# Causal beacon attention with a quick-GELU MLP on one core: direct loads of all values, whole scratch writes, a fixed order of products

## The chip, the cores and the metric

The kernel runs on one core of one Trainium2 chip. Time is the device time of one execution in microseconds. Of 13 executions of the kernel before the median is 384.38 us (381.3 to 387.05). The profile is of one execution of 385.87 us, whose span from the first to the last instruction is 384.2 us.

## The reference

There are 8 batches, 8 heads, 576 positions of 64 elements, and 16 beacon keys and values per head that stand ahead of the others and are seen by every query.

```python
k_all = np.concatenate([beacon_k, k], axis=2)      # (8, 8, 592, 64)
v_all = np.concatenate([beacon_v, v], axis=2)
scores = scale * np.matmul(q, k_all.transpose(0, 1, 3, 2))
scores = np.where(causal, -1000000000.0, scores)   # causal over the 576, beacons always seen
a = np.exp(scores - scores.max(-1, keepdims=True))
a /= a.sum(-1, keepdims=True) + 1e-09
attn_out = np.matmul(a, v_all)
x = attn_out.transpose(0, 2, 1, 3).reshape(4608, 512)
h = x @ w_in                                       # (4608, 2048)
out = (h * (1.0 / (1.0 + np.exp(-1.702 * h)))) @ w_out
```

All inputs and the output are float32 in memory; the kernel loads them to float16 and accumulates in float32.

## The kernel before

**Attention.** The work is cut in 32 steps, step i being one pair of heads of one batch (four steps a batch). Scores are made transposed: keys on partitions, queries in the free dimension. `qk_chunk` (line 355) makes them in four chunks for both heads of the pair, from kT and qT that hold one head in partitions 0 to 63 and the other in 64 to 127. `exp_chunk` (line 368, ScalarE) turns each chunk into E, and `mask_chunk` cuts the diagonal blocks on GpSimd (line 391) or VectorE (line 384). `av_half` (line 425) multiplies E with the values, whose tile vb has 64 columns of values beside 64 columns of ones, so that the sums come out of the same product. Then come the copy out of PSUM (`av_out`, line 436), the turn of the sums (`z_turn`, 448), the reciprocal (454), the turn back (`z_back`, 458) and the multiplication into xT (`norm`, 467). These are VectorE's, except that some copies go to ScalarE.

**MLP.** Tokens are cut in nine groups of 512. Group g has sixteen first products of four matmuls each (`mlp1`, 494), sixteen gelus on ScalarE (506) and four second products of sixteen matmuls (`mlp2`, 516), each followed by a copy and a store of 256 KB (`mlp2_out`, `mlp2_store`). A group may start when the batches that it holds are normalized. ScalarE loads another function table when it goes from exponentials to gelus and back.

**q and k.** For batches 0 and 1 they come in long rows (`load_qk6`, six positions in a row), and TensorE transposes them (`tr_pe`, 179) through PSUM with copies by `tr_pe_out` (187). For batches 2 to 7 VectorE turns 32 by 32 squares (`tr_squares`, 277), VectorE or GpSimd puts them in order (`tr_order`, 286), and SyncE writes the result to scratch memory (`tr_write`, 297) and reads it back to where it belongs (`tr_place`, 303).

**Values.** For batches 2 to 7 `load_v` (231) loads them with rows of one head and position. For batches 0 and 1 `load_v6` brings them in long rows into the tile of the second weight, which is not filled yet, and `v_pe` (204) sends each row to its partition by products with a 0/1 matrix (`spread`, made on GpSimd); beacon values are added by a product with the identity (208). Ten copies (226) bring them from PSUM to vb. The second weight's first three quarters wait for the last of these products.

**What sets the order.** All of the kernel is a list of `Work` items with an engine (or a choice), a planned duration, a key and the items that they need or follow. `issue` is a list scheduler: it repeatedly takes the item with the earliest planned start, counting engines, buffers (`Buf`, with `rings` as the numbers of buffers) and a planned DMA time, and so writes every engine's instruction order by hand ahead of the run. On the chip, engines run their orders strictly and wait on semaphores; the planned times decide nothing else. Items of key 1e6 are warm-up products (`warm`, 916) that fill planned gaps of TensorE. Loads are issued by GpSimd, whose masks stand in the same order; scratch transfers and stores are issued by SyncE. A load from GpSimd reuses one of eight semaphores, so it waits for the eighth before it.

A few lines that a sentence doesn't say:

```python
ends = [min(NPAIR * (((g + 1) * GT - 1) // S) + LAG, NSTEP) for g in range(NG)]   # 6 10 14 18 22 26 30 32 32
```

`ends[g]` is the step whose exponentials follow group g's gelus.

Of the kernel before, what the change touches and what calls it, by code (L numbers as in the profile page):

```python
# [9 lines left out]
F16 = mybir.dt.float16  # L10
# [6 lines left out]
def kernel(  # L17
# [34 lines left out]
    NBV = 2  # L52
# [27 lines left out]
    make_identity(nc, ident)  # L80
    keep = cst.tile([P, P + Nb], F16, tag="keep", name="keep")
    spread = cst.tile([TP, NKPAD + TR + 2], F16, tag="spread", name="spread")
    bkn = cst.tile([Nb, NB2, H, D], F16, tag="bkn", name="bkn")
    bvn = cst.tile([Nb, NBV, H, D], F16, tag="bvn", name="bvn")
# [13 lines left out]
    def make_spread():  # L98

        nc.gpsimd.affine_select(  # L100
            out=spread,
            in_=spread,
            compare_op=ALU.not_equal,
            fill=1.0,
            base=-Nb - TR,
            pattern=[[1, NKPAD + TR + 2]],
            channel_multiplier=-TR,
        )

# [9 lines left out]

# [3 lines left out]
    for t in kTs:  # L123
        nc.vector.memset(t[:, :, NK:NKPAD], 0.0)
# [21 lines left out]
    vflat = w2t.rearrange("p a n -> p (a n)")  # L146

    def load_qk6(b, g, w):
        if b not in nat6:
            nat6[b] = gp.tile([TP, 2, H, TR * D], F16, tag="g", name="g")  # L150
        nc.gpsimd.dma_start(
            out=nat6[b][:, w, g * HG : (g + 1) * HG, :],
            in_=(q, k)[w][b, g * HG : (g + 1) * HG].rearrange("h (p t) d -> p h (t d)", t=TR),
        )

    def v6(b):
        n = H * TR * D
        return vflat[0:TP, b * n : (b + 1) * n].rearrange("p (h t d) -> p h t d", h=H, t=TR)

    def load_v6(b):  # L160
        nc.gpsimd.dma_start(
            out=v6(b).rearrange("p h t d -> p h (t d)"),
            in_=v[b].rearrange("h (p t) d -> p h (t d)", t=TR),
        )

    def load_beacons(t, src):
        nc.gpsimd.dma_start(
            out=t.rearrange("n b h d -> n (b h) d"),
            in_=src[0 : t.shape[1]].rearrange("b h n d -> n (b h) d"),
        )  # L170
# [30 lines left out]

    vu = {}

    def v_pe(b, j):
        u = psu.tile([P, H * D], F32, tag="u", name="u")
        vu[(b, j)] = u
        if j == 0:
            nc.tensor.matmul(
                u[:, :],
                ident[0:Nb, :],  # L210
                bvn[:, b, :, :].rearrange("n h d -> n (h d)"),
                start=True,
                stop=False,
            )
        for t in range(TR):
            nc.tensor.matmul(  # L216
                u[:, :].rearrange("r (h d) -> r h d", h=H),
                spread[:, j * P - t + TR : (j + 1) * P - t + TR],
                v6(b)[:, :, t, :],
                start=(t == 0 and j > 0),  # L220
                stop=(t == TR - 1),
            )

    def v_pe_out(b, j, eng):
        r = min(P, NK - j * P)
        copy[eng](
            out=vbs[b % 2][0:r, j, :, 0:D],
            in_=vu[(b, j)][0:r, :].rearrange("r (h d) -> r h d", h=H),
        )

    def load_v(b, j, h0, h1):
        vb = vbs[b % 2]
        if j == 0:
            nc.gpsimd.dma_start(
                out=vb[0:Nb, 0, h0:h1, 0:D],
                in_=beacon_v[b, h0:h1].rearrange("h n d -> n h d"),
            )
            nc.gpsimd.dma_start(
                out=vb[Nb:P, 0, h0:h1, 0:D],
                in_=v[b, h0:h1, 0 : P - Nb, :].rearrange("h n d -> n h d"),  # L240
            )
        else:
            lo = j * P - Nb
# [50 lines left out]
    def tr_write(b, g, w, e):  # L294
        if e == 0:
            dqk[(b, g, w)] = dr.tile([2, P, QKW[w]], F16, tag=f"d{w}", name=f"d{w}")
# [654 lines left out]
```

The softmax here doesn't subtract the row's maximum and nothing guards it: scores larger than these inputs give would overflow.

## Time and profile before

| what | value |
|---|---|
| median of 13 executions | 384.38 us |
| the profiled execution | 385.87 us, span 384.2 us |
| TensorE busy | 367.9 us (96%) |
| VectorE busy | 266.5 us (69%) |
| ScalarE busy | 226.3 us (59%) |
| GpSimd busy | 146.5 us (38%) |
| scattering products of values (216) | 13.6 us in 60 matmuls |
| warm-up products (916) | 6.4 us in 18 matmuls |
| q0, the loads from GpSimd | 42816 packets, 18.62 MB |
| q1, SyncE's transfers | 18048 packets, 23.79 MB |

The engines are PE (TensorE), DVE (VectorE), ACT (ScalarE), POOL (GpSimd) and SP (SyncE). A busy time is the union of an engine's instructions in the profiled execution; ends of matmuls are modelled. PEclk is the granted clock of TensorE. A table by stage gives, for each stretch, the busy time and number of instructions of each engine, then the clock, the busy share of 16 DMA engines, and what they moved. In the chain of waits each row is a start, a duration, and an engine with the tile and line that it worked on.

### The profile page before, as it was taken

The numbers are of one execution on the slowest core, as the hardware profiler recorded it, in microseconds if no ns is written. First come the engines' busy times: TensorE is split into PE (matmuls) and PEld (weight loads), VectorE is DVE, ScalarE is ACT, GpSimd is POOL, SyncE is SP. The second block draws the span as 40 slices with busy tenths as digits, with TensorE's granted clock in tenths as the row PEclk, the third lists the DMA queues.
The fourth block names the chain that finished last, engine by engine and source line by source line (L and its number), as shares of the span: only waits on it lengthen the run. The fifth ranks groups of instructions, "written<-read, shape, count | busy, mean of one in ns | idle before, by whom it ended". The sixth has DMA issues, their size and how long they took to land.

```text
span 384.2 us, 6119 instructions
## 1 busy us (share of the span) xinstructions
PE 367.9 (96%) x2328; PEld 181.2 (47%) x2328; DVE 266.5 (69%) x443; ACT 226.3 (59%) x334; POOL 146.5 (38%) x263
## 2 busy tenths in 40 slices
PE   7897999889999999999999999999999999999995
PEld 3454445434445444444445774545444544444442
DVE  6468999389977997699859985998595458000021
ACT  1876866627674777477746766586648563735300
POOL 8455772326533752466235724472321030000000
PEclk9998999989999999999999999999999999999999
DMA  8999998746955794559465947494400011000012
GB/s 110 200 205 154 135 180 118 167 142 116 130 138 137 142 129 128 149 116 149 128 158 95 156 118 178 89 147 108 143 27 30 0 56 46 10 27 27 15 68 82
DMA packets 60892, 42.79 MB, mean 111 GB/s; under 512 B 32192, under 2 KB 53184, under 8 KB 60864
## 3 DMA queue, kind: packets, MB, share of 16 engines
q0 software_dynamic: 42816, 18.62, 40.8%
q1 hardware_dynamic: 18048, 23.79, 20.3%
q8 instruction: 18, 0.29, 0.3%
q14 instruction: 10, 0.08, 0.1%
HBM read 44.40 MB, written 16.61 MB: 159 GB/s over the span
## 4 chain that ended last, share of the span: by engine, by line
PE 58%; DVE 28%; ACT 7%; issue 3%; DMA 3%; POOL 0%; SPq 0%; ACTq 0%; DVEq 0%
PE u L494 28%; PE u L516 18%; DVE xT L467 6%; DVE zt L448 6%; PE u L425 5%; DVE O L436 5%; ACT E L368 4%; PE s L355 3%; DVE sq L277 3%; DVE rz L458 3%; ACT L368 2%; DVE osb L529 2%; PE u L216 2%; PE u L916 2%; DMA n<-in_k_dram 1%
## 5 line engine op out<-in xcount | busy, mean ns | idle before, releaser
L368 ACT ACTIVATE E<-s 128x1024 f16<-128x1024 f32 (+3 forms) x128 | 104.0, 867 | 60.4 <-PE s L355 35.4
L494 PE MATMUL u<-xT,w 128*128 128x512 f16 (+1 forms) x640 | 133.6, 358 | 2.5 <-DVE O L436 1.6
L516 PE MATMUL u<-w,g 128*128 128x512 f16 x576 | 131.1, 383 | 2.8 <-DVE O L436 2.8
L506 ACT ACTIVATE g<-u 128x512 f16<-128x512 f32 x144 | 83.9, 598 | 53.0 <-PE u L494 52.9
L391 POOL TENSOR_SCALAR_AFFINE_SELECT E<-E 128x256 f16<-128x256 f16 (+2 forms) x147 | 58.4, 415 | 132.2 <-ACT E L368 131.6
L494 PEld LDWEIGHTS <-w 128*128 128x128 f16 x640 | 60.2, 98 | 60.1 <-issue 6.7
L516 PEld LDWEIGHTS <-g 128*128 128x128 f16 x576 | 55.1, 99 | 68.9 <-issue 5.4
L529 DVE COPY osb<-u 128x512 f32<-128x512 f32 x30 | 20.4, 681 | 74.9 <-PE u L516 74.8
L425 PE MATMUL u<-E,vb 128*128 128x336 f16 (+4 forms) x448 | 56.5, 270 | 0.8 <-DVE qT L187 0.7
L436 DVE COPY O<-u 128x240 f32<-128x240 f32 (+1 forms) x103 | 42.2, 432 | 14.9 <-PE u L425 13.4
L467 DVE TENSOR_TENSOR xT<-O,rz 64x576 f16<-64x576 f32 x64 | 51.8, 810 | 0.8
L448 DVE STREAM_TRANSPOSE zt<-O 64x576 f32<-64x576 f32 x64 | 49.3, 770 | 1.7 <-ACT O L436 0.2
L425 PEld LDWEIGHTS <-vb 128*128 128x128 f16 (+1 forms) x448 | 38.7, 99 | 20.7 <-issue 4.7
L355 PE MATMUL s<-qT,kT 64*128 64x80 f16 (+5 forms) x384 | 39.1, 284 | 3.8 <-ACT E L368 2.5
L286 POOL COPY t<-sq 128x576 f16<-128x576 f16 x24 | 29.1, 1211 | 32.0 <-DVE sq L277 31.6
L277 DVE STREAM_TRANSPOSE sq<-n 128x576 f16<-128x576 f16 x48 | 35.2, 752 | 4.7 <-POOL E L391 3.5
L355 PEld LDWEIGHTS <-kT 64*128 64x128 f16 x384 | 14.3, 94 | 33.1 <-issue 26.1
L286 DVE COPY t<-sq 128x576 f16<-128x576 f16 x24 | 27.3, 1136 | 0.2
L458 DVE STREAM_TRANSPOSE rz<-rt 128x576 f32<-128x576 f32 x32 | 24.4, 764 | 0.5
L245 POOL DMA_DIRECT2D vb<-in_v_dram x24 | 21.3, 893 | 0.0
L216 PE MATMUL u<-w,spread 96*128 96x512 f16 x60 | 13.6, 380 | 0.0
L436 ACT COPY O<-u 128x336 f32<-128x336 f32 (+1 forms) x25 | 10.4, 424 | 2.4 <-PE u L425 2.2
(49 smaller groups left out, 128.9 us busy)
## 6 DMA issues: line engine op xcount, KB each, us to landing
out_dram<-osb SPq DMA_DIRECT2D x36, 256.0 KB
d<-t SPq DMA_DIRECT2D x24, 148.0 KB
kT<-d SPq DMA_DIRECT2D x12, 296.0 KB
n<-in_k_dram POOLq DMA_DIRECT2D x12, 288.0 KB, 4.2
n<-in_q_dram POOLq DMA_DIRECT2D x12, 288.0 KB, 5.2
d<-t SPq DMA_DIRECT2D x24, 144.0 KB
qT<-d SPq DMA_DIRECT2D x12, 288.0 KB
vb<-in_v_dram POOLq DMA_DIRECT2D x18, 128.0 KB, 5.9
```

Source lines behind the costliest of these rows:

```text
L277: nc.vector.transpose(sqs[(b, g, w)][:, c * n : (c + 1) * n, :, :], nat[(b, g, w)][:, c * n : (c + 1) * n, :],)
L286: copy[eng](out=tqk[(b, g, w)][:, e, o : o + S].rearrange("p (r t) -> p r t", t=TPP), in_=sqs[(b, g, w)][:, :, e, :].rearrange("p t r -> p ...
L355: nc.tensor.matmul(sc[:, x, o : o + e - a], kT[r : r + 64, p, j * P : (j + 1) * P], qT[r : r + 64, p, a:e], start=True, stop=True,)
L368: nc.scalar.activation(out=Es[i][:, :, choff[ci] : choff[ci] + w], in_=scs[(i, ci)][:, :, 0:w], func=AFT.Exp, scale=0.125,)
L391: nc.gpsimd.affine_select(out=blk, in_=blk, compare_op=ALU.is_ge, fill=0.0, base=mc, pattern=[[0, 2], [1, w]], channel_multiplier=-1,)
L425: nc.tensor.matmul(u[:, lo:hi], vb[0:kw, j, :, :].rearrange("r h c -> r (h c)")[:, o : o + 2 * D], E[0:kw, x, col : col + hi - lo], start= ...
L436: copy[eng](out=Os[i][:, x, AQ[half] : AQ[half + 1]], in_=avu[(i, x, half)][:, :])
L448: nc.vector.transpose(zst[i][0][64 * x : 64 * x + 64, :, :], Os[i][64 * (1 - x) : 64 * (1 - x) + 64, x, :])
L467: vec[eng].tensor_tensor(out=xT[r : r + 64, p, c : c + S], in0=Os[i][r : r + 64, x, :], in1=zst[i][2][r : r + 64, :], op=ALU.mult,)
L494: nc.tensor.matmul(u[:, o : o + w], w1t[:, kp, nt * P : (nt + 1) * P], xT[:, kp, m : m + w], start=(kp == 0), stop=(kp == NKP - 1),)
L506: nc.scalar.activation(out=gts[g][:, nt, :], in_=hu[(g, nt)][:, :], func=AFT.Gelu_apprx_sigmoid)
L516: nc.tensor.matmul(o[:, :], gts[g][:, nt, mt * P : (mt + 1) * P], w2t[:, nt, :], start=(nt == 0), stop=(nt == NNT - 1),)
```

## The change

It has five parts.

1. The values of batches 0 and 1 are loaded by `load_v` like all others. `spread`, `load_v6`, `v_pe`, `v_pe_out`, the beacon-value load into bvn and the second weight's wait go.
2. A scratch write takes both halves (e = 0, 1) of a group in one transfer, with 128 partitions as its slowest dimension; the scratch layout and the reading in `tr_place` follow. Within a head the 64 elements come in another order, the same one for q and k.
3. q and k of batch 0 come in six loads (heads 0 to 1, 2 to 3, 4 to 7), those of batch 1 in two. The identity, the mask matrix and the beacon keys become planned items, and the order of the first memsets changes.
4. The plan has other numbers: DMA times, latencies, a bias for the choice between ScalarE and VectorE, and an added rule that a transfer starts no earlier than 2.0 us after the landing of the eighth before it.
5. TensorE's order is fixed around the MLP groups by `chain`: all sixteen first products together (for groups 1 to 6 with nothing of a step between them), and one second product in each of the four steps ahead of the next group. `ends` becomes a list with a step more for groups 1 to 6.

```diff
-            out=nat6[b][:, w, g * HG : (g + 1) * HG, :],
-            in_=(q, k)[w][b, g * HG : (g + 1) * HG].rearrange("h (p t) d -> p h (t d)", t=TR),
+            out=nat6[b][:, w, h0:h1, :],
+            in_=(q, k)[w][b, h0:h1].rearrange("h (p t) d -> p h (t d)", t=TR),
...
-    def load_v(b, j, h0, h1):
+    def load_v(b, j):
         vb = vbs[b % 2]
+        lo = max(0, j * P - Nb)
+        hi = min((j + 1) * P - Nb, S)
+        r = Nb if j == 0 else 0
         if j == 0:
             nc.gpsimd.dma_start(
...
+                out=vb[0:Nb, 0, :, 0:D], in_=beacon_v[b].rearrange("h n d -> n h d")
+            )
+        nc.gpsimd.dma_start(
+            out=vb[r : r + hi - lo, j, :, 0:D],
+            in_=v[b, :, lo:hi, :].rearrange("h n d -> n h d"),
+        )
...
-    def tr_write(b, g, w, e):
-        if e == 0:
-            dqk[(b, g, w)] = dr.tile([2, P, QKW[w]], F16, tag=f"d{w}", name=f"d{w}")
+    def tr_write(b, g, w):
+        dqk[(b, g, w)] = dr.tile([2, P, QKW[w]], F16, tag=f"d{w}", name=f"d{w}")
         nc.sync.dma_start(
-            out=dqk[(b, g, w)].rearrange("l (y e r) s -> e (l y) r s", y=2, e=2)[e],
-            in_=tqk[(b, g, w)][:, e, QKO[w] :],
+            out=dqk[(b, g, w)].rearrange("e p s -> p e s"), in_=tqk[(b, g, w)][:, :, QKO[w] :]
         )
...
-            in_=dqk[(b, g, w)].rearrange("l p s -> p l s"),
+            in_=dqk[(b, g, w)].rearrange("e (l m) s -> m e l s", l=2),
...
-    SEM = 0.1
+    SEM, QS = 0.1, 0.1
+    SPL, CAP = 2.5, 2.0
...
+    midn = Work("POOL", 0.6, -5.95, lambda: make_identity(nc, ident))
+
+    bk6 = Work("POOL", 0.57, -5.97, load_bk6, dma=0.25)
...
+        for (h0, h1) in ((0, 2), (2, 4), (4, H)) if b == 0 else ((0, H),):
...
-        if b < NBV:
-            first_values(b)
-            continue
+        kv = 4 * b - 1.5 if b >= NB2 else (-5.5, -3)[b]
         for j in range(NJ):
...
-            "POOL", 0.75, 4.2 + 0.01 * c, lambda c=c: load_w2(c),
-            vpe[-1:] if 2 * c < 3 * NBV else [], dma=3.0,
+            "POOL", 0.78, 4.2 + 0.01 * c, lambda c=c: load_w2(c), dma=2.55,
...
-    ends = [min(NPAIR * (((g + 1) * GT - 1) // S) + LAG, NSTEP) for g in range(NG)]
+    ends = [6, 11, 15, 19, 23, 27, 31, 32, 32]
...
-        k0 = ends[g] - 0.4 + 2 * max(0, g - 7)
+        k0 = ends[g] - 1 + 2 * max(0, g - 7)
...
+    def chain(*ws):
+        for x, y in zip(ws, ws[1:]):
+            y.after.append(x)
+
+    for g in range(NG):
+        e, nxt = ends[g], (ends + [NSTEP])[g + 1]
+        if e == NSTEP:
+            break
+        chain(qks[(e - 1, 3)], *m1s[g])
+        m2 = {i: m2s[(g, n)] for n, i in enumerate(range(max(e, nxt - GT // P), nxt))}
+        seq = [m1s[g][-1]] + avp[e - 1][:2]
+        seq += [m2[e]] if e in m2 else []
+        seq += [qks[(e, 2)], qks[(e, 3)]]
+        seq += avp[e - 1][2:]
+        for i in range(e + 1, nxt):
+            seq += [qks[(i, 0)], qks[(i, 1)], *([m2[i]] if i in m2 else []), qks[(i, 2)], qks[(i, 3)]]
+            seq += avp[i - 1]
+        if nxt < NSTEP:
+            seq.append(m1s[g + 1][0])
+        else:
+            seq += avp[nxt - 1] + [m2s[(g, 3)]]
+        chain(*seq)
...
+                t = max(t, landed[eng][-8] + CAP)
```

## The prediction

> **What bounds the kernel now.** I read the page's busy shares first, then its slices.
>
> ```profile
> span 384.2 us, 6119 instructions
> PE 367.9 (96%) x2328; PEld 181.2 (47%) x2328; DVE 266.5 (69%) x443; ACT 226.3 (59%) x334; POOL 146.5 (38%) x263
> ...
> PE   7897999889999999999999999999999999999995
> ...
> DMA  8999998746955794559465947494400011000012
> ```
>
> TensorE is busy nearly throughout; the digits under 9 lie in the first ten slices, where the DMA row is full too. That asks for a table by stage. I cut it at the first product of the MLP (47.86), at the second group's MLP (94) and where the last two groups begin (325.5):
>
> ```profile
> core 0: us, PE busy (x) PEld busy (x) DVE busy (x) ACT busy (x) POOL busy (x), PEclk, DMA share, GB/s
> 0.00:47.86 47.86, 41.65 (x399) 21.59 (x399) 33.99 (x57) 31.51 (x50) 30.57 (x62) 0.96 1.09 161
> 47.86:94.00 46.14, 42.49 (x265) 19.86 (x262) 38.19 (x64) 25.66 (x37) 20.25 (x33) 0.96 0.79 143
> 94.00:325.50 231.50, 229.05 (x1418) 115.07 (x1418) 188.77 (x316) 149.15 (x217) 95.67 (x170) 1.00 0.61 113
> 325.50:384.20 58.70, 54.74 (x253) 24.63 (x252) 5.54 (x8) 20.02 (x33) 0.00 (x0) 0.99 0.11 41
> ```
>
> From 94 to 325.5 TensorE idles 2.45 us: nothing can be won there but its own work, which stays the same. The last stage idles 3.96, nearly all of it the last copy and store. So the head decides. The same table for the scattering product of the first values (line 216) has one row that isn't zero, and the chain of waits shows what it does:
>
> ```profile
> 0.00:47.86 47.86, 13.64 (x60) 5.55 (x60) 0.96 1.09 161
> ```
> ```profile
> 2.52 6.36 PE u L916 x18
> ...
> 10.97 1.89 ACT E L368 x2
> ...
> 15.40 6.58 PE u L216 x30
> ...
> 22.75 0.83 PE u L425 x7
> 23.60 0.83 DVE O L436 x2
> 24.46 0.78 DVE zt L448
> ...
> 44.87 0.76 DVE xT L467
> ```
>
> The first exponentials are there at 11 us, but the first product with values (line 425) comes at 22.7, behind 30 scattering products. From there VectorE carries the chain (copies, turns, normalizing) until batch 0 is normalized at 45.6, which the first MLP product needs.
>
> So I split the span into TensorE work that both kernels have, and the rest. Busy 367.93, less warm-up products 6.36 (line 916), line 216's 13.64 and the two beacon-value products of line 208 (0.77 over the same stage) is **347.16 useful**. The rest is 37.0: 26.98 before the first MLP product (6.36 + 14.41 + idle 6.21), 3.65 to 94, then 2.45 and 3.96.
>
> **The change, part by part.**
>
> *Scattering removed.* TensorE loses 14.41 us, ScalarE nine copies of 0.59 and VectorE one of 0.65. Before the first MLP product this is no gain in itself: TensorE waits there for others, and 20.9 of 47.9 us are useful work. What counts is when the chain starts.
>
> *Values direct.* Batch 0's values come in six transfers queued behind the first q and k loads of heads 0 to 3, batch 1's behind the first weight. They have rows of 128 bytes in place of 768. Their price, from the DMA answers for 10 to 20 us (768-byte rows) and for 56.8 to 59.8 us (mostly 128-byte rows):
>
> ```profile
> DMA packets 2665, 2.00 MB, mean 200 GB/s; under 512 B 77, under 2 KB 2664, under 8 KB 2664
> ```
> ```profile
> q0 software_dynamic: 2602, 0.37, 177.8%
> ```
>
> 266 long rows a us against about 850 short ones. A batch has 4608 + 128 short rows, 5.5 us, against 768 long ones, 2.9. The Trainium skill (DMA: Bandwidth & Descriptors, Specifications) speaks against the change here: it asks for at least 512 bytes for full rate. The row agrees and sizes it: +2.6 us a batch. The same page's fit (2.0 us and bytes at 436 GB/s; "Anatomy of one DMA") would charge 1.18 MB of source 2.7 us, no penalty at all. GpSimd's wait for the eighth transfer back shows that batch 0's values land at 14.8 now (its third load of the first weight starts at 14.80, released by them). In the new queue the loads of heads 4 to 7 (768 rows, 2.9 us), the old value load (2.9) and the beacon values (0.3) are no longer ahead, and 5.5 are: 14.8 − 6.1 + 5.5 = 14.2. GpSimd has issued them by about 10 (five loads of 0.57 to 0.8 from 1.8, six of 0.55 to 0.9), and its shortest value load lands in 3.6 us, so issue isn't later. Step 0's third and fourth exponentials run from 13.26 (0.95 and 0.53), the last mask takes 0.41: 15.1. ScalarE's new order reaches them no earlier, with four copies of 0.66 first. So the first product with values starts at **15.2, 7.5 us earlier**. By the fit the values would land at 12.5, and the masks would still say 15.2.
>
> *What follows in the queue.* Heads 4 to 7 (2.9) land at 17.1, batch 1's q and k (5.8) at 22.9, the first weight (2.1 MB at those 200 GB/s, 10.3) at 33, batch 1's values at **38.6** (36 by the fit). They are needed by the first half of step 4, just ahead of the first MLP product. The second weight, no longer waiting for the scattering (whose input lay in its tile), lands after batch 2's q and k by about 55.
>
> *Eight in flight.* The wait was there before:
>
> ```profile
> POOL w L252 <- DMA w<-in_v_dram: 5.2, 2, 3.0
> ```
>
> The plan now counts it, but GpSimd still stands in it, and masks stand behind. By the new order step 1's last two masks come behind the third of batch 1's value loads, which waits for batch 1's k at 20: masks at 21.7. VectorE has 6.1 us of step 0 (copy 0.43, turns 2 × 0.77, two kT copies 1.5, reciprocal 0.27, turn 0.77, two multiplies 1.6) from 15.9, to 22.0: covered. Step 3's last masks wait for the third quarter of the first weight at about 31; step 3's exponentials end near 30.8: covered within 1 us.
>
> *First MLP product.* From the first product with values to it takes 25.2 us now (22.68 to 47.86), on VectorE's chain. Tracing VectorE's new order over its four steps gives copies 1.3, turns 6.2, reciprocals 1.1, turns back 3.1, multiplies 6.5 and q/k copies 4.3: 22.5, and about 1.5 of waits. I keep 25.2, since batch 1's values allow no start under 39.5: 15.2 + 25.2 = **40.4**. Useful work ahead of it is the same 20.9: the order has 24 more transposes (+0.8) and 8 more score products (+0.85), 12 fewer with values (−1.65). The rest there is 19.6 instead of 27.0: **−7.4**.
>
> *Fixed order.* After group 0's MLP products the order has half a step with values, 12 warm-ups, scores, half a step, scores, then the second MLP product; before, that came at once and hid ScalarE's table load. Now: last gelu 0.7, table load 1.28, exponential 1.03, the next 0.95, and two more scores behind the third and fourth, in all 6.0 us, of which 2.6 useful: 3.4 lost. Against that, the 2.76 us idle near 76 us (VectorE stuck behind a transpose whose buffer GpSimd held) have no place in the new order. With 0.8 at the table load ahead: 4.2 for 3.65, **+0.6**. For groups 1 to 6 all 64 first products stand together, with no step among them. VectorE's orders there: 13.7 us of its work stand in the 13.9 us of products, leaving 20.2 of the 33.9 us that it is busy between 133.6 and 172.8 for the other 25.3. I take 0; bounds −0.3 (all idle gone) and +1.5 a group (two 0.75 us turns ahead of a copy that frees TensorE's buffer). The later ends put two second products (7.2 us) behind the last step instead of one (3.6), over its 5 us chain: **−0.5**.
>
> *Scratch writes.* The rows are as many and as long; SyncE issues 24 fewer of 0.52 us.
>
> ```profile
> SPq L303 <- DMA d<-t: 78.0, 30, 7.0
> ...
> PEld L355 <- DMA kT<-d: 0.2, 1, 0.2
> ```
>
> SyncE waits 2.6 us per placing for the write, but TensorE waits 0.2 us in all for what is placed. The page's "How many engines (k)" gives the old pattern (slowest dimension 4) four engines and the new one (128) sixteen; the trace doesn't show the split. I take 0; hidden under a lead of some us. Without that lead the writes would be worth those 2.6.
>
> *Identity and mask* move ahead of or among the loads: 0.3 us later for the first, while its half size (two heads) gives about as much back: 0.
>
> **Sum.** 384.2 − 7.4 + 0.6 − 0.5 = 376.9 span. The profiled execution took 385.87, 1.67 more than its span, and lies 1.49 over the median: 376.9 + 0.2 = **377.1 us**.
>
> **Rivals.** *Head hidden behind the loads:* where short rows share the engines with other traffic, batch 1's values come at 600 a us, not 850 (+2.3 each), and step 1 to 3 masks wait with the queue. Then the first MLP product starts at about 46, and the time is about 383. For it: a DMA row at 9 in the head, GpSimd already waiting; against: in the head nothing else runs. *Fixed order stalls (slower):* where a turn pair stands ahead of buffer-freeing copies, TensorE has no other product to take. At 1.5 us in each of seven groups, 10.5: 387.6; it decides from 1.05 a group on. For it: VectorE at 82% from 94 to 325; against: the 5 us spare above. *Better still:* the first MLP product at 38 and no half-clock windows (0.96 in both head stages, 3.7 us of lost product time at most): 371.5. *The direct loads do nothing*, as VectorE's chain starts late anyway: excluded by 22.7, unless masks hold it.
>
> **From cases to numbers.** Forecast 0.52 (own range 373 to 381), loads 0.20 (380 to 387), stalls 0.20 (384 to 392), better 0.08. A half percent, 1.9 us, is what this measurement can tell. Faster: 0.52 + 0.08 + 0.04; same: 0.12 of the loads; slower: 0.20 + 0.04. The range leaves out half of the best case and the end of the stalls: 371 to 388.
>
> **What would show it.** Line 425's counterpart starting at 15 to 16 instead of 22.7; the first MLP product near 40; the idle and warm-up time before it under 20; no more than 0.6 us TensorE idle a group after 94; TensorE waiting for VectorE's output copies there would prove the stalls, and GpSimd waits on loads beyond 8 us with late masks the load rival.

## The result and the profile after

The changed kernel takes 378.33 us (median of 11 executions, 376.8 to 379.84) against 385.31 us for the kernel before (48 executions); the ratio is 0.984, 95% interval 0.981 to 0.987. The forecast was 377.1, so the time was right within 1.2 us. The sum behind it wasn't: two terms that I had put at nothing are worth several microseconds, and one that came in as worked out is lost again before it reaches the end.

The page of the changed kernel (span, busy shares, then the slices of TensorE, of its clock and of the DMA engines):

```profile
span 374.9 us, 6003 instructions
PE 357.6 (95%) x2290; PEld 176.7 (47%) x2290; DVE 255.0 (68%) x421; ACT 231.5 (62%) x345; POOL 156.2 (42%) x271
...
PE   8976999689999999999999999999999999999995
PEclk9996999969999999999999999999999999999999
DMA  8999999969459963797469745941010011000012
```

All that is under 9, but for the last slice, still lies in the first ten, but there are two dips, in the fourth slice and in the eighth, and the clock row shows slices of lower clock in the fourth and ninth. The second dip lies where the head should be over.

The table by stage, cut at the same events as before (first MLP product 40.14, second group's first 91.89, last two groups 315.58), and the warm-up products (line 865) in the first two stages:

```profile
0.00:40.14 40.14, 32.65 (x368) 16.79 (x369) 28.50 (x46) 29.43 (x48) 31.89 (x63) 0.91 1.55 158
40.14:91.89 51.75, 46.88 (x278) 22.31 (x275) 41.37 (x72) 30.40 (x45) 31.11 (x50) 0.93 1.21 172
91.89:315.58 223.69, 222.69 (x1395) 112.69 (x1393) 178.94 (x296) 152.54 (x222) 93.21 (x160) 1.00 0.57 112
315.58:374.90 59.32, 55.42 (x257) 24.95 (x255) 6.23 (x9) 19.11 (x32) 0.00 (x0) 1.00 0.11 40
```
```profile
0.00:40.14 40.14, 10.61 (x30) 3.13 (x30) 0.91 1.55 158
40.14:91.89 51.75, 2.75 (x12) 1.11 (x12) 0.93 1.21 172
```

The first MLP product is 7.7 us earlier than before (40.14 for 47.86). The second group's comes at 91.89, where it was 92.66. That isn't quite the same place, since one attention step more is done by then, but the stage between is 51.75 us long with a clock of 0.93, and holds 4.87 us without a matmul. The waits (engine, tile and line, who released it, microseconds in all, times, longest) name it:

```profile
DVE sq L211 <- DMA n<-in_k_dram: 4.4, 1, 4.4
...
PE u L359 <- DVE osb L463: 3.9, 2, 3.6
```

The chain of waits (start, duration, what) shows the head as predicted, and then the one place where the end hangs on a load again:

```profile
20.25 0.89 POOL vb L179
21.14 0.64 POOL E L325
21.82 0.93 PE u L359 x8
...
40.21 2.77 PE u L428 x12
...
58.84 12.00 DMA n<-in_k_dram
70.87 0.78 DVE sq L211
71.64 0.72 DVE O L370 x2
...
76.13 0.59 DVE osb L463
76.76 1.24 PE u L359 x5
```

A k load of batch 3, issued at 58.84, lands 12 us later. VectorE's turn of it (line 211) stands ahead of the copies of the running step, so TensorE's next values wait 3.62 us for a buffer. A cut of the same stage at that wait shows the second half of the price, in the column after the busy times (the clock):

```profile
72.90:76.76 3.86, 0.24 (x5) 0.12 (x2) 3.80 (x8) 0.34 (x1) 1.93 (x2) 0.82 0.36 77
76.76:82.20 5.44, 5.44 (x21) 2.05 (x21) 4.75 (x9) 1.89 (x2) 4.38 (x7) 0.50 0.60 106
82.20:91.89 9.69, 9.69 (x69) 4.94 (x68) 7.52 (x15) 4.91 (x8) 5.48 (x12) 1.00 1.37 143
```

TensorE works 5.44 us at half clock, which is 2.7 us of lost products. So the stall costs about 3.6 + 2.7 = 6.3 us. The lead of 7.7 is nearly gone.

For the experiments a table that doesn't depend on where groups stand is of more use: the start of a step's first exponential (ScalarE runs four a step, in order, in every kernel here), taken from the records of each profiled execution. Steps 15 to 31 are four groups of the middle.

| kernel | median, us | ratio to before (95%) | step 6 | step 11 | step 15 | steps 15 to 31 | span |
|---|---|---|---|---|---|---|---|
| before | 385.31 | | 67.1 | 117.6 | 156.9 | 157.1 | 384.2 |
| after | 378.33 | 0.984 (0.981 to 0.987) | 57.4 | 107.8 | 146.9 | 153.0 | 374.9 |
| b_direct | 388.56 | 1.006 (1.002 to 1.010) | 68.0 | 120.0 | 159.2 | 156.5 | 386.0 |
| b_direct_plan | 385.28 | 1.002 (0.998 to 1.006) | 64.3 | 117.1 | 156.4 | 156.5 | 383.2 |
| b_one_write | 382.45 | 0.990 (0.981 to 0.998) | 67.3 | 113.4 | 152.6 | 157.4 | 380.2 |
| b_fixed_order | 392.77 | 1.022 (1.017 to 1.028) | 64.6 | 118.2 | 158.2 | 154.7 | 388.0 |
| b_fixed_one_write | 377.98 | 0.981 (0.971 to 0.991) | 64.2 | 108.1 | 146.9 | 154.7 | 376.6 |
| a_two_writes | 383.67 | 0.994 (0.990 to 0.998) | 60.2 | 110.4 | 151.4 | 154.8 | 381.2 |
| a_early_k | 378.38 | 0.983 (0.975 to 0.990) | 60.2 | 110.4 | 148.7 | 152.8 | 376.5 |
| a_late_turn | 371.29 | 0.960 (0.954 to 0.967) | 58.4 | 103.0 | 141.5 | 153.2 | 369.7 |
| a_old_ends | 387.78 | 1.009 (1.004 to 1.014) | 57.9 | 109.3 | 148.8 | 160.8 | 384.6 |
| a_free_later | 394.12 | 1.025 (1.018 to 1.032) | 60.7 | 115.9 | 157.4 | 163.2 | 393.9 |
| a_free_order | 397.08 | 1.029 (1.023 to 1.035) | 60.1 | 118.0 | 158.8 | 163.8 | 396.4 |
| a_free_old_lat | 401.23 | 1.042 (1.033 to 1.051) | 59.6 | 114.6 | 156.3 | 165.8 | 398.4 |

Names with a_ are edits of the changed kernel, names with b_ of the kernel before. No kernel leaves out or changes any of the computation. Two kernels can be compared by step only where their groups follow the same steps: after, b_fixed_order, b_fixed_one_write, a_two_writes, a_early_k and a_late_turn do; the stretch from step 15 to 31 holds 989 matmul records in all of these, 992 in before, b_one_write and the three a_free kernels, and 1011 in a_old_ends. Ratios stand against runs of the kernel before on the same chip, and the rows were measured on several chips: where two rows differ by a few microseconds, their ratios and the step columns say more than their medians. Ratios leave out slow executions (those over 1.5% above the fastest of their kernel), and so do the medians of the edited kernels; with them a_free_order has 400.64, b_fixed_order 394.1 and b_fixed_one_write 378.15, the figures that some of the expectations below name.

### The profile page after: what moved, and what is told of

Read it like the earlier page. It is cut to its first block, busy times and chain, and to the rows that moved or that the text cites. A ratio compares the mean times of both kernels' runs of the same rounds, so it can differ in the third digit from the quotient of the medians.

```text
span 374.9 us, 6003 instructions
## 1 busy us (share of the span) xinstructions
PE 357.6 (95%) x2290; PEld 176.7 (47%) x2290; DVE 255.0 (68%) x421; ACT 231.5 (62%) x345; POOL 156.2 (42%) x271
## 4 chain that ended last, share of the span: by engine, by line
PE 76%; DVE 10%; DMA 6%; ACT 3%; POOL 3%; issue 1%; POOLq 0%; ACTq 0%
PE u L428 33%; PE u L450 28%; PE u L359 8%; PE s L289 5%; DMA n<-in_k_dram 3%; ACT E L302 3%; DVE zt L382 3%; DMA g<-in_k_dram 2%; DVE xT L401 2%; DVE O L370 2%; POOL vb L179 1%; DVE t L220 1%; POOL g L130 1%; DVE rz L392 1%; DVE sq L211 1%
## 5 line engine op out<-in xcount | busy, mean ns | idle before, releaser
L428 PE MATMUL u<-xT,w 128*128 128x512 f16 (+1 forms) x640 | 126.6, 358 | 0.0
L325 POOL TENSOR_SCALAR_AFFINE_SELECT E<-E 128x256 f16<-128x256 f16 (+2 forms) x153 | 66.1, 450 | 88.1 <-ACT E L302 87.8
L428 PEld LDWEIGHTS <-w 128*128 128x128 f16 x640 | 61.9, 98 | 60.6 <-issue 1.1
L463 DVE COPY osb<-u 128x512 f32<-128x512 f32 x29 | 19.9, 686 | 67.7 <-PE u L450 67.3
L370 DVE COPY O<-u 128x240 f32<-128x240 f32 (+1 forms) x88 | 36.8, 439 | 32.3 <-PE u L359 29.6
L359 PEld LDWEIGHTS <-vb 128*128 128x128 f16 (+1 forms) x448 | 37.8, 99 | 28.5 <-issue 15.2
L220 POOL COPY t<-sq 128x576 f16<-128x576 f16 x18 | 23.7, 1316 | 47.4 <-DVE sq L211 42.5
L289 PE MATMUL s<-qT,kT 64*128 64x80 f16 (+5 forms) x384 | 37.3, 288 | 3.3 <-ACT E L302 1.5
L179 POOL DMA_DIRECT2D vb<-in_v_dram x40 | 35.3, 887 | 7.6 <-DMA w<-in_moe_w_out_dram 3.9
L289 PEld LDWEIGHTS <-kT 64*128 64x128 f16 x384 | 13.0, 95 | 26.9 <-issue 20.4
L370 ACT COPY O<-u 128x336 f32<-128x336 f32 (+1 forms) x40 | 15.5, 426 | 7.2 <-PE u L359 7.1
L865 PE MATMUL u<-wu 128*128 128x512 f16 x42 | 13.4, 459 | 1.3 <-DVE wu L857 1.3
```

The costliest lines, as they stand in the source:

```text
L179: nc.gpsimd.dma_start(out=vb[r : r + hi - lo, j, :, 0:D], in_=v[b, :, lo:hi, :].rearrange("h n d -> n h d"),)
L220: copy[eng](out=tqk[(b, g, w)][:, e, o : o + S].rearrange("p (r t) -> p r t", t=TPP), in_=sqs[(b, g, w)][:, :, e, :].rearrange("p t r -> p ...
L289: nc.tensor.matmul(sc[:, x, o : o + e - a], kT[r : r + 64, p, j * P : (j + 1) * P], qT[r : r + 64, p, a:e], start=True, stop=True,)
L325: nc.gpsimd.affine_select(out=blk, in_=blk, compare_op=ALU.is_ge, fill=0.0, base=mc, pattern=[[0, 2], [1, w]], channel_multiplier=-1,)
L359: nc.tensor.matmul(u[:, lo:hi], vb[0:kw, j, :, :].rearrange("r h c -> r (h c)")[:, o : o + 2 * D], E[0:kw, x, col : col + hi - lo], start= ...
L370: copy[eng](out=Os[i][:, x, AQ[half] : AQ[half + 1]], in_=avu[(i, x, half)][:, :])
```

## Experiments: one part undone, one part alone

**The fixed order taken out of the changed kernel.** The chains go, and the list of steps goes back to the formula; the transfers, their order and the plan's numbers stay.

```diff
-    ends = [6, 11, 15, 19, 23, 27, 31, 32, 32]
+    ends = [min(NPAIR * (((g + 1) * GT - 1) // S) + LAG, NSTEP) for g in range(NG)]
...
-        k0 = ends[g] - 1 + 2 * max(0, g - 7)
+        k0 = ends[g] - 0.4 + 2 * max(0, g - 7)
...
-        chain(qks[(e - 1, 3)], *m1s[g])
...
-        chain(*seq)
```

> The kernel after with the fixed order taken out (the old list of ends, no chain); values direct, scratch writes and plan stay. Theory A (the head gives most of the 9.3 us of span): first product with values still near 14 us, first MLP product near 40 us, but TensorE's first products of the MLP in groups of 4 and 8 again, so their busy time goes from 126.6 us back to about 133: 381 to 384 us. Theory B (the fixed order gives most): 384 us or more, whatever the head does. If the order costs nothing: 378 us, and idle TensorE after 92 us stays at 1 us.

It took 397.08 us, far above theory A: the order that I had charged +0.6 us and nothing for the middle is worth 19 us against this plan left free. Step 6 is reached at 60.1, 7 us ahead of the kernel before; each later stage is slower than in that kernel (steps 6 to 11 57.9 for 50.5, 11 to 15 40.8 for 39.3, 15 to 31 163.8 for 157.1). So the changed plan and the fixed order belong together, and undoing one part says little on what that part is worth in the kernel before. Parts had to be tried there as well.

**The fixed order alone in the kernel before.** The same chains and the same list of steps, with scattered values and two scratch writes.

```diff
-    ends = [min(NPAIR * (((g + 1) * GT - 1) // S) + LAG, NSTEP) for g in range(NG)]
+    ends = [6, 11, 15, 19, 23, 27, 31, 32, 32]
...
+        chain(qks[(e - 1, 3)], *m1s[g])
...
+        chain(*seq)
```

> The kernel before with the fixed order alone (ends, chain). Theory A: the head is as before (first product with values at 22.7 us), the busy time of the first products falls by about 6 us: 378 to 381 us, less if the gap after the first group is paid here too (2 to 3 us). Theory B: 378 us or less. If the contiguous products are not what shortened the middle: 384 us.

392.77 us, slower, where all three expectations had it faster or level, though four groups of the middle are 2.4 us shorter than before. One wait of TensorE, and the clock after it, take away more than that (waits, then a table of two stretches):

```profile
PE s L355 <- DMA qT<-d: 7.9, 1, 7.9
```
```profile
73.70:81.60 7.90, 0.00 (x0) 0.02 (x1) 3.69 (x8) 0.00 (x0) 0.22 (x1) 0.63 0.40 99
81.60:86.00 4.40, 4.39 (x17) 1.62 (x18) 1.21 (x2) 1.89 (x2) 2.59 (x6) 0.50 0.65 151
```

The fixed order wants batch 2's q from scratch memory at 73.7, for step 8, and q isn't there until 81.6. The kernel before comes to step 8's exponentials at 84.3 only. The lead of "some us" under which I hid the scratch path had been made by the order that the change removes.

**Direct values alone, twice.** First with the values' loads exchanged and the rest as it was, then with the changed kernel's costs of transfers and its limit of eight in the plan's first 40 us too.

```diff
-    NBV = 2
+    NBV = 0
...
-                (4 * b - 1.5 if b >= NB2 else -3.9) + 0.1 * j,
+                (4 * b - 1.5 if b >= NB2 else (-4.89, -3)[b]) + 0.1 * j,
```

> The kernel before with the direct values alone; the old plan, that knows of no limit of eight loads, puts the first weight and all of batch 1's value loads ahead of step 0's first GpSimd mask. Theory C (direct loads need the limit in the plan): the mask waits for the second quarter of the first weight at about 27 us, step 1's product with values comes at 28 us instead of 21: 381 to 386 us. Theory A alone (the head gains as soon as values are direct): 377 to 379 us.

388.56 us, slower than expected, and for another reason. The first product with values starts at 27.06 instead of 22.7: it waits for nothing there; the plan, which counts a transfer at its old price of 2.2 us, has put warm-up products ahead of it.

```diff
+                if w.dma and t < 40:
+                    t = max(t, landed[eng][-8] + 2.0)
...
-                dma_free[eng] = max(dma_free[eng], t + d + 0.7) + w.dma
-                w.t1 = dma_free[eng] + (1.0 if t < 12 else dict(SP=4.0, POOL=2.0)[eng])
+                dma_free[eng] = max(dma_free[eng], t + d + (1.6 if t < 40 else 0.7)) + w.dma
+                w.t1 = dma_free[eng] + (0.4 if t < 40 else dict(SP=4.0, POOL=2.0)[eng])
```

> The kernel before with direct values and, for planned times under 40 us, the new DMA costs and the rule of eight loads in flight; old order of products, old scratch writes, old latencies after 40 us. Theory C (direct values pay once the plan places them): first product with values at 15 to 17 us instead of 27, first MLP product at 40 to 42 us, the middle as before: 376 to 380 us. If the gain is only the fixed order's: 384 us or more.

With those numbers the first product with values comes at 14.88, and still the time is that of before, 385.28, where 376 to 380 was expected. Step 9 comes 6.7 us earlier than before (83.8 for 90.5), step 10 only 0.6 (110.9 for 111.5). In between VectorE waits 5.1 us for a k load, at 78.5 to 83.6, TensorE waits 2.9 us in two pieces (1.5 and 1.4), and a half clock of 6.8 us begins at 88.3. Direct values with these plan numbers, and nothing else, bring nothing that can be measured.

**The single write alone, and with the fixed order.** The kernel before with the changed `tr_write` and `tr_place`; then the same with the chains and the list of steps.

```diff
-            out=dqk[(b, g, w)].rearrange("l (y e r) s -> e (l y) r s", y=2, e=2)[e],
-            in_=tqk[(b, g, w)][:, e, QKO[w] :],
+            out=dqk[(b, g, w)].rearrange("e p s -> p e s"), in_=tqk[(b, g, w)][:, :, QKO[w] :]
...
-                for e in range(2):
-                    wr.append(Work(
-                        "SP", 0.45, k0, lambda b=b, g=g, w=w, e=e: tr_write(b, g, w, e),
...
+                wr = Work(
+                    "SP", 0.55, k0, lambda b=b, g=g, w=w: tr_write(b, g, w), cp + need, alloc=db_,
```

> The kernel before with the single scratch write over all queues alone; values scattered, order left to the plan. Theory P (the write pays only where the fixed order leaves the scratch path no lead): 383.5 to 386.5 us, within 0.5% of before. Rival W (the write pays by itself, as in the changed kernel, where two writes cost 5.3 us): 378 to 382 us.

> The kernel before with the fixed order and the single scratch write; values scattered and plan numbers as before. Theory D (the fixed order leaves no lead for the scratch path, and the single write gives it back): the one 7.9 us wait of TensorE for qT near 74 us shrinks by 5 us or more, 384 to 388 us instead of 394. If the writes don't matter: 393 to 395 us and the same wait.

The write alone gives 382.45 us (0.990, 0.981 to 0.998): faster than theory P's 383.5 to 386.5, and just outside rival W's 378 to 382. Together with the fixed order it gives 377.98, better than expected and the whole gain of the change, with the values still scattered. The wait for q is gone: step 9 comes 10.2 us earlier than in b_fixed_order (80.1 for 90.3).

What a write costs, the DMA view shows. A stretch of the middle from just after a pair of writes is issued to the reading that waits for them, in the kernel before (busy tenths of 16 engines in 40 slices, then what they moved):

```profile
DMA  6998824364142222222239999988887758997999
GB/s 115 181 165 148 148 33 82 75 108 58 25 58 58 76 101 85 101 93 76 93 91 225 216 210 292 219 195 219 219 225 233 184 94 96 123 128 124 187 210 204
```

And of the same batch's write in one transfer:

```profile
DMA  9395590220300769989999999999997999979821
GB/s 213 71 390 106 106 354 0 36 36 0 71 0 0 198 219 382 327 291 328 364 346 291 328 328 383 310 360 434 325 446 289 428 352 473 441 284 347 315 95 63
```

Before, there is a stretch of digits 2, about a quarter of sixteen engines, at some 60 to 100 GB/s; after, nines at 300 GB/s and more. From the writes' issue to the reading's it is 129.52 to 135.24 before, 5.7 us, and 125.28 to 127.92 here, 2.6 us. The packet records of the two traces say the same: of the writes' packets (1184 bytes) four are under way at a time in that stretch, and some sixteen with the single write. This fits the Trainium skill's rule (DMA: Bandwidth & Descriptors, "How many engines (k)") that I had quoted with four and sixteen. I had also written that the trace doesn't show the split. It does, in this view.

**Two writes in the changed kernel.** The other way round, with the order's numbers as they are.

```diff
-        nc.sync.dma_start(
-            out=dqk[(b, g, w)].rearrange("e p s -> p e s"), in_=tqk[(b, g, w)][:, :, QKO[w] :]
-        )
+        for e in range(2):
+            nc.sync.dma_start(
+                out=dqk[(b, g, w)].rearrange("l (y e r) s -> e (l y) r s", y=2, e=2)[e],
+                in_=tqk[(b, g, w)][:, e, QKO[w] :],
+            )
```

> The kernel after with the old scratch writes (two transfers of 148 KB per group with a slowest dimension of 4, old layout), same orders on all engines. Theory A (they are hidden): 378 us within 1 us, with SyncE's waits for the write up from now to about 80 us. Rival: one of the placings comes late and TensorE waits for kT or qT: over 380 us.

383.67 us, above theory A's 378: 5.3 more by the medians, 4.0 by the two ratios. TensorE's wait for q is back, at 69.5 to 75.1:

```profile
PE s L291 <- DMA qT<-d: 5.6, 1, 5.6
```

SyncE's wait for writes, 78.0 us in the kernel before, is 102.8 here (32 times), and with one write, in the changed kernel,

```profile
SPq L237 <- DMA d<-t: 44.4, 16, 5.4
```

The changed kernel comes to step 8's exponentials at 67.3, 17 us earlier than the kernel before. With one write SyncE issues the reading of batch 2's first q at 54.3, with two at 66.9.

This wait is not what makes the difference in time, though. Steps 6 to 11 take 50.2 us here and 50.4 in the changed kernel: the late q stands in the place of the changed kernel's stall for k. Of the 6.3 us between the two profiled executions, 2.8 are there by step 6; the half clock begins already at 9.8 us, long before the first scratch write (45.3), so this part can't be put down to the writes. The rest comes at step 15 (1.9) and step 19 (1.6), where TensorE waits 1.9 and 1.7 us for VectorE's copies. Ahead of the first of these VectorE has stood 1.8 us in the turn of a k load, one of two such waits (3.3 us) that the changed kernel doesn't have there.

## Experiments: where the lead of the values goes

After these runs the changed kernel (378.33) stands level with b_fixed_one_write (377.98), which has no direct values at all. By step 6 it is 6.8 us ahead (57.4 for 64.2), by step 11 it is 0.3 ahead. What lies between is the k load of batch 3.

**The k load earlier.** The first loads of batch 3's k and q may go a step earlier, batch 2's values a step later.

```diff
-                late.append((Lq[(b, g, w)], 4 * b + 2 * g - 6))
+                late.append((Lq[(b, g, w)], 4 * b + 2 * g - 6 - (b == 3 and g == 0)))
...
-            late.append((V[(b, j)], 4 * b - 3))
+            late.append((V[(b, j)], 4 * b - 3 + (b == 2)))
```

> The kernel after with batch 3's first k and q loads allowed a step earlier and batch 2's values a step later, so that k is issued ahead of the values. Theory E (VectorE stood 4.4 us in a turn whose load lay behind batch 2's values, and TensorE 3.6 us behind VectorE, with 6.8 us of half clock after it): TensorE's longest wait after 60 us under 1 us, 371 to 375 us. If the stall has another cause: 378 us with a wait of over 3 us in the same place.

378.38 us: no gain, where 371 to 375 was expected. The load is issued at 47.4 and lands at 64.8, 17 us later; the plan moves VectorE's turn forward with it, and VectorE stands 4.55 us at 60.3 to 64.8. The queue is full to 72 us, so an earlier load only waits longer in it. TensorE still waits 2.9 us, at 69.8, and a half clock of 6.8 us follows from 71.3. The stall moved; steps 6 to 11 take 50.2 us for 50.4.

**The turn later.** Loads as they are; only VectorE's turns of this k and q are tied to a later step's exponentials, so that the copies of the running step stand ahead of them.

```diff
+    for w in (1, 0):
+        for x in turns[(3, 0, w)]:
+            x.needs.append(exps[9][0 if w else 3])
```

> The changed kernel, with VectorE's turns of batch 3's first k and q tied to step 9's exponentials, about a step later in VectorE's order; the loads and all else are as they were. Theory S (the lead of the direct values is lost because VectorE stands 4.43 us behind a k load that landed at 70.87, TensorE then 3.62 us behind VectorE's copy, and a half clock of 6.8 us follows): VectorE stands under 1 us at 58 to 82, TensorE's wait at 72 and the half clock after it go, group 1's first product comes at 86 to 89 instead of 91.89, the time is 371 to 375 us. Rival Q (the full load queue holds something else of this stretch, or the batch is then late on the scratch path): TensorE waits as long at another place, group 1 at 91 to 93, the time 377 to 380 us.

371.29 us (0.960, 0.954 to 0.967), as theory S expected, and the fastest kernel of all. The k load takes as long as ever (12.4 us from issue to landing), and nobody waits for it. VectorE in that time (start, duration, line, operation):

```profile
66.42 1.20 DVE L370 COPY O<-u 128x240 f32<-128x240 f32 x3
67.54 1.56 DVE L382 STREAM_TRANSPOSE zt<-O 64x576 f32<-64x576 f32 x2
...
73.61 1.57 DVE L382 STREAM_TRANSPOSE zt<-O 64x576 f32<-64x576 f32 x2
75.20 0.78 DVE L211 STREAM_TRANSPOSE sq<-n 128x576 f16<-128x576 f16 x1
```

where the changed kernel has

```profile
66.04 0.40 DVE L370 COPY O<-u 128x240 f32<-128x240 f32 x1
70.87 0.78 DVE L211 STREAM_TRANSPOSE sq<-n 128x576 f16<-128x576 f16 x1 [4.43 <-DMA n<-in_k_dram]
```

Its second stage is 45.95 us long, with the clock at 1.00 (the stage of the changed kernel: 51.75 and 0.93):

```profile
41.16:87.11 45.95, 44.60 (x286) 21.94 (x283) 42.56 (x73) 31.27 (x47) 32.12 (x52) 1.00 1.28 188
```

So the stall was worth 6 to 7 us: 7.0 by the medians, 6.2 by the starts of the steps after step 6 (1.0 us behind the changed kernel there, 5.2 ahead at step 31), 6.3 as worked out above. With no stall on either side, the kernel with direct values takes 6.9 us of span less than the one with scattered values (369.7 for b_fixed_one_write's 376.6): 5.8 by step 6, 5.1 by step 11, and 1.5 more in the four groups. This is the size that the forecast gave the head. It is not the direct values' alone, since the loads of the first q and k and the plan's numbers differ between these two kernels as well; the split of those loads was never tried by itself.

**The same load in the kernel before.** It has a stall at the same load, and my prediction misread it. VectorE, before the change:

```profile
73.29 0.69 DVE L529 COPY osb<-u 128x512 f32<-128x512 f32 x1 [2.38 <-PE u L516]
77.50 0.78 DVE L277 STREAM_TRANSPOSE sq<-n 128x576 f16<-128x576 f16 x1 [3.52 <-POOL E L391]
```

The releaser named is a mask of GpSimd. In b_one_write GpSimd's order and its masks' times are the same to 0.3 us, its last mask ends at 77.7, and the transpose runs at 74.15, ahead of it:

```profile
73.54 0.69 DVE L529 COPY osb<-u 128x512 f32<-128x512 f32 x1 [2.38 <-PE u L516]
74.15 0.77 DVE L277 STREAM_TRANSPOSE sq<-n 128x576 f16<-128x576 f16 x1
```

What differs is the load. Issued at 68.50 and 68.75, it took 8.9 us before and 4.8 with the single write; before, SyncE's scratch traffic (q1 moved 0.96 MB in those 8.9 us) was still running when it started. So the transpose waited for its k (68.50 + 8.9 = 77.4), and a mask happened to end at 77.5. That is where the write alone gains: 2.8 us of TensorE's idle time and a half clock of 3.4 us after it are gone, and steps 6 to 11 take 46.1 us for 50.5.

## Experiments: what the fixed order does

**The steps as they were.** The fixed order stays, groups 1 to 6 come a step earlier.

```diff
-    ends = [6, 11, 15, 19, 23, 27, 31, 32, 32]
+    ends = [6, 10, 14, 18, 22, 26, 30, 32, 32]
```

> The changed kernel with the fixed order as it is, but groups 1 to 6 one step earlier, as before (6, 10, 14, 18, 22, 26, 30). It tells the two halves of the fixed order apart. Theory C (the gain comes from the sixteen first products standing together): 377 to 381 us, the 448 first products of groups 1 to 7 at 84 us as before this edit. Rival L (the step more is what makes a contiguous group possible, since the last normalized outputs of its batch are ready then): TensorE waits 1 to 3 us at each of six groups, half clocks follow, 384 to 395 us.

387.78 us, as rival L expected. In five groups TensorE issues the first four or eight products, then waits 0.7 to 0.8 us for VectorE to finish the multiplication of the last step; in a sixth it waits 1.0 and 2.3 us:

```profile
PE u L428 <- DVE xT L401: 7.2, 7, 2.3
```

Another 2.9 us is a wait for the second weight, whose products now come a step earlier, and a half clock of 3.4 us follows each of these two long waits. The 160.8 us of steps 15 to 31 are no measure of the loss, since 22 more matmuls lie in that stretch; TensorE is idle 3.8 us in it, and 0.5 in the changed kernel. Products that stand together leave TensorE nothing else to do when the group's input is late, and the step more is what makes it early.

**The later steps without the chains.** The fourth of the four combinations.

```diff
-        chain(qks[(e - 1, 3)], *m1s[g])
...
-        chain(*seq)
...
-        k0 = ends[g] - 1 + 2 * max(0, g - 7)
+        k0 = ends[g] - 0.4 + 2 * max(0, g - 7)
```

> The changed kernel without the fixed order but with the step more before groups 1 to 6 kept. With the fixed order and the step more 378.3, with the fixed order and the old steps 387.8, with neither 400.6 us. Theory L (the step more is what counts, the order only hardens it): 378 to 385 us, and the idle time of some 2 us per group in the middle is gone. Rival C (both are needed: a planner left free spreads the first products over the steps again, whichever step the gelus follow): 390 to 402 us.

394.12 us, as rival C expected. With the changed plan's numbers: neither 397.1, the steps alone 394.1, the chains alone 387.8, both 378.3. Each helps by itself, and neither suffices.

**Old latencies in the free order.** Perhaps the new plan counts transfers as landing too early after the head.

```diff
-                    dma=1.4,
+                    dma=1.8,
...
-                w.t1 = f + dict(SP=SPL, POOL=0.4 if t < 40 else 1.0)[eng]
+                w.t1 = f + dict(SP=SPL if t < 40 else 4.0, POOL=0.4 if t < 40 else 2.0)[eng]
```

> The kernel after with no fixed order, as in the run that took 400.6 us, but with the old longer latencies (2.0 us for loads, 4.0 for scratch transfers) and the old DMA time of q and k loads for planned times over 40 us. Theory F (the free order went wrong because the new numbers plan loads to land too early, so that VectorE stands in turns of q and k): VectorE's waits for k loads fall from 16 us to under 5, 380 to 386 us. If the order itself is at fault: 395 us or more.

401.23 us: the theory falls. VectorE's waits for k loads go down from 23.8 us to 5.1, and TensorE's waits spread over exponentials, masks and VectorE's parts of E instead. Why this plan, left free, makes 164 us of four groups where the plan before makes 157, stays open. It is not that the first products are spread: in a_free_order a first product is followed by another line's only 4 times in that stretch, as in the changed kernel (24 times in the kernel before), and yet TensorE is idle 8.1 us for 1.6 before. The costs of the other transfers, the choice between ScalarE and VectorE and the limit of eight were not tried one by one.

**Why it pays in the middle.** From b_one_write to b_fixed_one_write only the order and the steps change, and four groups go from 157.4 to 154.7 us. The groups of instructions, before the order is fixed and after (line 494, all first products):

```profile
L494 PE MATMUL u<-xT,w 128*128 128x512 f16 (+1 forms) x640 | 133.6, 358 | 2.5 <-DVE O L436 1.6 <-DVE xT L467 0.6
```
```profile
L494 PE MATMUL u<-xT,w 128*128 128x512 f16 (+1 forms) x640 | 126.3, 358 | 0.4 <-DVE O L436 0.4
```

The same 640 products are busy 7.3 us less, and waited 2.1 us less. Not all of it is gained: when lines alternate, one stretch of time can count for both, and TensorE's whole busy time falls by 4.7 us (366.3 to 361.6). In steps 15 to 31 it is busy 2.8 us less (155.4 to 152.6) and idle as long as before (1.9 and 2.0), so all of the gain there is busy time. In the same stretch a run of first products gives way to another line's 4 times for 24. What a change of lines costs in itself no run here shows. This is the work that the prediction called "its own work, which stays the same". The changed kernel's other 1.7 us there are idle time (0.5 us for 2.0); which of its other parts saves them was not tried.

## Why the prediction was right, and where it wasn't

**The head was right.** Measured, with the forecast in brackets: first product with values 14.19 (15.2), step 1's held products at 21.82 behind the mask and the eighth load, by the way that I had given (21.7), first MLP product 40.14 (40.4), rest ahead of it 40.14 − 32.65 + 10.61 = 18.1 (19.6). That scattering's 14.4 us of TensorE are no gain in themselves was right. The 850 short rows a microsecond, on which the order of landing rests, gave milestones right within 1 us.

**"Against that, the 2.76 us idle near 76 us … have no place in the new order"** failed, and with it the +0.6 of that stage. The 6.0 us gap at the table load was right (5.6, from 55.31 to 60.92). But the stall near 76 was a late k load, not a buffer that GpSimd held; the new order has the same turn at the same place, and fuller queues ahead of the load. Measured: 3.62 us of wait where I took none, and 2.7 of half clock; the stage's rest is 51.75 − 46.88 + 2.75 = 7.6 us where I had 4.2.

**"Scratch writes. I take 0; hidden under a lead of some us"** failed. The single write is worth 3 to 4 us alone (382.45; ratio 0.990) and 4 to 5 in the changed kernel. The fallback, 2.6 us a placing "without that lead", was near the one pair that was compared (5.7 − 2.6 = 3.1 us from issue to reading). What two writes cost TensorE came by two ways: in the kernel before, a k load from GpSimd's queue landed 4.1 us later beside them; under the fixed order, q itself came late (7.9 us).

**"For groups 1 to 6 … I take 0"** was mis-sized: four groups take 4.1 us less than before (157.1 to 153.0), 2.4 of them by the order alone. The bounds of −0.3 to +1.5 us a group left room for a loss of that size and for a gain of idle time only, none for busy time.

**The tail** was right in kind: 59.32 − 55.42 = 3.9 us, where the kernel before, cut at the same product (324.42), has 4.2. That is −0.3; I had −0.5.

**The sum.** The forecast's span was 376.9, the measured one 374.9, and the profiled execution here lies 1.7 us under its median, where that of before lay 1.5 over the median of its 13. In the prediction's terms, span fell by 9.3 us: the rest ahead of the first MLP product by 8.9 (forecast 7.4), the rest of the second stage rose by 4.0 (0.6), idle time behind it fell by 1.5 (0.5), and useful work, which was to stay, fell by 2.9 with 2.7 us of half clock still in it. So the agreement of 377.1 with 378.33 is in part luck: two gains of several microseconds that were put at nothing, a loss of 6 to 7 that was put at 0.6, and 3 us of difference between profiled executions and medians stand against each other.

**The rivals.** Loads that hide the head: no, by 40.14. Its sign, though, was there: GpSimd's waits for the eighth load back sum to 12.5 us, beyond the 8 that I named,

```profile
POOL vb L179 <- DMA w<-in_moe_w_out_dram: 3.9, 2, 2.8
POOL n L114 <- DMA w<-in_moe_w_in_dram: 2.7, 2, 1.3
POOL n L114 <- DMA w<-in_moe_w_out_dram: 2.2, 1, 2.2
POOL vb L179 <- DMA w<-in_moe_w_in_dram: 2.0, 2, 1.2
POOL vb L179 <- DMA g<-in_k_dram: 1.7, 1, 1.7
```

and yet TensorE waited for masks 1.4 us in all. GpSimd's waits were no sign of a late head. Fixed order stalls: the order does stall (b_fixed_order, 392.77), but as one wait for a load and its clock, not as a turn ahead of the copies in every group. The best case, 371.5, asked for no half clock and a first MLP product at 38 (by its own terms, 377.1 − 2.4 − 3.7, it would be 371.0); a_late_turn gets to 371.29 with that product at 41.16 and a half clock of 6.8 us in the head, so that its agreement is one of numbers only.

## What to carry to other kernels

A part that makes one stage earlier is worth only what the next fixed engine order lets through: follow it to the next instruction that stands in order behind a load, and ask when that load lands under the new traffic. Parts of a change that look independent can need one another: here the fixed order alone costs 2%, the single write alone gives 1%, and together they give 2%. Where a releaser named by the profile had no reason to hold the instruction, look up when its own input landed before believing the name.

## What the runs showed of the hardware

**A short stall can cost a half clock behind it, in pieces of 3.4 us, and its length alone doesn't decide.** TensorE's idle time and the half clock in the records after it: 2.8 us in the kernel before, then 3.4; 2.9 in a_early_k, then 6.8; 3.6 in the changed kernel, then 6.8; 5.6 in a_two_writes, then 6.8; 7.9 in b_fixed_order, then 10.2. In these the half clock begins 1.5 to 3.0 us after the wait does, so that a part of it can fall into a long wait. But 2.65 us in a_old_ends was followed by none, and the same wait of 3.74 us, at the same place ahead of the last groups, left a_free_order at full clock (its products start 216 ns apart) and cost a_free_old_lat 6.8 us of half clock (427 ns apart). The Trainium skill (TensorE: Matmul & The Clock Gate, the two states of Part 1) gives half clock after an idle window of about 3.4 us; the pieces of 3.4 us are in these records, but here an idle time of 2.8 us was enough once and one of 3.7 us was not.

**A load's latency is that of the traffic around it.** The same k load of 288 KB took 4.8 us in b_one_write, 8.9 in the kernel before, with scratch writes still under way on SyncE's queue, 12.0 in the changed kernel, issued after the second weight and batch 2's values, and 17.4 in a_early_k, issued earlier still.
